# A planned single-core kernel: q and W1 loaded ahead of the filter, DFT angles built on VectorE, new planner numbers

## The chip, the cores and the metric

The kernel runs on one core of one Trainium2 chip. A core has five engines with an instruction queue each: TensorE (PE, with its weight loads as PEld), VectorE (DVE), ScalarE (ACT), GpSimd (POOL) and SyncE (SP), which here only issues transfers (DMAs). The metric is the device time of one execution in microseconds (us); less is better.

## What is computed

Two branches read x = q (2048 rows of 640, bfloat16) and are mixed by a gate. Branch A shifts k along the rows with a 4-tap filter, multiplies by v, convolves each column with a filter as long as the sequence (by FFT in the reference) and multiplies by q. Branch B is a layernorm, a matmul with W1, gelu, a shift of rows by column group, W2, a residual, another layernorm, and a W3-gelu-W4 block.

```python
g = _sigmoid((x * gate_w).sum(-1, keepdims=True))
kv = k_shift * v                                   # k_shift: 4 taps over k
y = irfft2(rfft2(pad(kv)) * rfft2(pad(ssm_k)))[:S] # long convolution
a = q * (y + kv * ssm_D)
h = _gelu(_layernorm(x) @ w1)
x1 = x + shifted(h) @ w2                           # column groups shifted by 1, -1, 2, -2 rows
b = x1 + _gelu(_layernorm(x1) @ w3) @ w4
return g * a + (1 - g) * b
```

## The kernel before

Rows are handled in 16 slabs of 128 (row = 16 p + slab). The long convolution is a DFT in two steps done as matmuls. Step 1 (line 783) multiplies the tables F1 (cosines and sines, interleaved by column) with a slab: first of the filter HT ("h1", 16 slabs by 2 halves), later of the product kv ("x1"). Step 2 (line 899) is a set of 64-wide matmuls with the small tables M3, after the data have been written to GHD or GXD in DRAM and read back in another layout; the spectra are multiplied on DVE (959), pass step 2 backwards into VD, and the inverse step 1 ("iv", 995) uses I1, the transposed F1.

The filter arrives as five tiles RG of 128 columns (line 400) and is transposed on PE (761); five evictions on ACT or DVE (379, 383) fill HT, and every step-1 matmul of the filter needs all five. HT shares its memory with KV: v of slabs 4c to 4c+3 may be loaded (859) only after step 1 of those slabs has read HT. The shifted-key products on DVE (870, 875, 879, 882) turn v into kv.

Branch B: for each slab statistics (on DVE 556 and 557, or on ACT 560 and 561, two passes with an accumulated sum), then on POOL the reciprocal root for a pair of slabs (573 to 579), then the normalisation on DVE (586), a transpose on PE (601), W1 (634) in four chunks of four slabs with five groups of five matmuls each and the gate's small matmuls (639, 643), gelu on ACT (652, 655), W2 (728), the residual on DVE (735), the second layernorm whose transposes are DMAs (593), W3 (815), gelu (819), W4 (827) and a residual (833).

The tables: F1[t1] holds cos and sin of an angle proportional to (column + 1) times row number. POOL writes index tables (432), DVE converts them (439), and for each of 16 t1 either DVE (453, one instruction of 256 columns) or POOL (456, two of 128) makes angle = column * row + offset, the offset 6144 or 4096 for the even and odd columns. DVE takes each group of four modulo 8192 (461), ACT takes the sine (463). M3 is made likewise by POOL and ACT (494 to 518).

Nothing is issued in written order. The function builds nodes, each with the engines that may run it and an assumed cost, and a planner (`Plan.schedule`) list-schedules them: each engine takes the node with the lowest rank, a rank being the latest start by the chain behind it, capped by the due times in the table PAR; it also picks the engine, the buffers and the PSUM slot (four slots ps0 to ps3). So any change of a cost or of PAR reorders all queues. Each engine then runs its queue strictly in that order, also where its first instruction has to wait.

Of the kernel before, what the change touches and what calls it, by code (L numbers as in the profile page):

```python
# [12 lines left out]
ALU = mybir.AluOpType  # L13
# [25 lines left out]
DMA_ISSUE = 60.0  # L39
# [185 lines left out]
def act_s(n):  # L225
    return 95.0 + 0.833 * n


def dve(n, r=1.04):
# [7 lines left out]
    "keep": (0.07,), "evac": (1.85,), "vpen": (43.36,), "mpen": (14.32,),  # L237
# [4 lines left out]
def kernel(  # L242
# [67 lines left out]
    BPI = big.tile([P, 1], F32, name="BPI")  # L310
# [115 lines left out]
    NANG = GEN[:, 0:8192].bitcast(I32)  # L426
    wci, wcf = gt_(256, I32), gt_(256, F32)
    oci, ocf = gt_(256, I32), gt_(256, F32)
# [5 lines left out]
    i_w = pl.add("iw", {G: 400}, iota_fn(wci, [[128, 2], [2, 64], [0, 2]], 1))  # L434
    i_s = pl.add("is", {G: 200}, iota_fn(s16i, [[1, T1]], 0, T1))
    i_o = pl.add("io", {G: 400}, iota_fn(oci, [[0, 2], [0, 64], [-2048, 2]], 6144))

    def vcopy(o, i):
        return lambda e: nc.vector.tensor_copy(out=o, in_=i)

    c_w = pl.add("cw", {V: 200}, vcopy(wcf, wci), [i_w])
    c_s = pl.add("cs", {V: 90}, vcopy(s16, s16i), [i_s])
    c_o = pl.add("co", {V: 200}, vcopy(ocf, oci), [i_o])
    m_bpi = pl.add("bpi", {V: 70}, lambda e: nc.vector.memset(BPI[:], -PI))
    f1n = []
    for g in range(4):
        st = []
        for j in range(4):
            t1 = 4 * g + j
            def f_ang(e, t1=t1):  # L450
                o = NANG[:, t1 * 256:(t1 + 1) * 256]
                if e == V:
                    nc.vector.scalar_tensor_tensor(out=o, in0=wcf, scalar=s16[:, t1:t1 + 1], in1=ocf, op0=ALU.mult, op1=ALU.add)
                else:
                    for x in range(2):
                        nc.gpsimd.tensor_scalar(out=o.rearrange("p (j c) -> p j c", c=2)[:, :, x],
                                                in0=wcf.rearrange("p (j c) -> p j c", c=2)[:, :, x], scalar1=s16[:, t1:t1 + 1],
                                                scalar2=6144.0 - 2048.0 * x, op0=ALU.mult, op1=ALU.add)
            st.append(pl.add("ang%d" % t1, {V: 397, G: 700}, f_ang, [c_w, c_s, c_o]))
        n1 = NANG[:, g * 1024:(g + 1) * 1024]  # L460
        an = pl.add("and%d" % g, {V: dve(1024, .6)}, lambda e, n1=n1: nc.vector.tensor_scalar(
            out=n1, in0=n1, scalar1=8191, scalar2=None, op0=ALU.bitwise_and), st)
        f1n.append(pl.add("sin%d" % g, {A: act_s(1024)}, lambda e, g=g, n1=n1: nc.scalar.activation(
            out=F1[:, :, 4 * g:4 * g + 4, :].rearrange("p h a c -> p a h c"),
            in_=n1.rearrange("p (a h c) -> p a h c", a=4, h=2), func=ACT.Sin,
            scale=PI / 4096, bias=BPI[:]), [an, m_bpi], mode="sin"))

# [24 lines left out]
    def f_m3c(e):  # L492
# [24 lines left out]
        out=sn3, in_=ani, func=ACT.Sin, scale=PI / 8, bias=BPI[:]), [m3b, m_bpi], mode="sin")  # L517
# [24 lines left out]
    n_misc = pl.add("misc", {G: 600}, f_misc)  # L542
# [7 lines left out]
    def ln_slab(i, s, dep):  # L550
        s0 = s & ~1

        def f_st(e):
# [4 lines left out]
            else:  # L558
                if i == 0:
                    nc.scalar.activation(out=JNK if i else JN0, in_=QX[:, s, :], func=ACT.Copy, accum_out=SSM[:, s:s + 1])  # L560
# [482 lines left out]
```

## Time and profile before

| | us |
|---|---|
| median of 3 runs (lowest, highest) | 255.62 (255.55, 255.73) |
| the profiled execution | 254.59 |
| its span, first to last instruction | 252.8 |
| PE busy | 223.6 |
| DVE busy | 194.6 |
| ACT busy | 154.2 |
| POOL busy, all of it in the first 100 us | 59.3 |

A busy time is the time in which an engine had an instruction running. In rows of the timeline the columns are start, duration, engine, line, operation, output and input, and in brackets the idle time before it and what ended that. SPq is the queue of transfers.

### The profile page before, as it was taken

How to read it: one execution, taken by the hardware profiler on the slowest of the kernel's cores; microseconds unless marked ns; L12 is line 12 of the kernel's file. 1: busy time of each engine (PE TensorE's matmuls, PEld its weight loads, DVE VectorE, ACT ScalarE, POOL GpSimd, SP SyncE). 2: the span in 40 equal slices, each digit the busy share in tenths (PEclk: the TensorE clock that was granted, in tenths of full speed). 3: DMA queues.
4: the chain of work that ended last, by engine and by line, in shares of the span. 5: the costliest groups of instructions: out<-in, count | busy, mean ns of one | idle time of the engine just before them, and what ended most of it. 6: DMA issues, size and time to landing. Idle time of an engine off the chain costs nothing.

```text
span 252.8 us, 4384 instructions
## 1 busy us (share of the span) xinstructions
PE 223.6 (88%) x1628; PEld 129.9 (51%) x1645; DVE 194.6 (77%) x308; ACT 154.2 (61%) x210; POOL 59.3 (23%) x144
## 2 busy tenths in 40 slices
PE   3858949999799999898698999969899999999993
PEld 3816535575467644664344446525334554557662
DVE  5889779996999999969987117876829785147995
ACT  2689949996579865676486564576868457231000
POOL 8899884122434880000000000000000000000000
PEclk9986997999999999999799999997999999999999
DMA  7998972279999962189999869958999243799973
GB/s 261 389 363 283 356 269 90 52 221 393 370 202 174 263 265 26 37 200 327 367 385 306 327 210 243 299 184 264 370 352 392 80 164 107 240 367 337 396 232 136
DMA packets 50069, 65.10 MB, mean 258 GB/s; under 512 B 19584, under 2 KB 36737, under 8 KB 49664
## 3 DMA queue, kind: packets, MB, share of 16 engines
q1 hardware_dynamic: 50048, 64.82, 80.1%
q8 instruction: 13, 0.21, 0.3%
q14 instruction: 8, 0.07, 0.1%
HBM read 37.03 MB, written 18.35 MB: 219 GB/s over the span
## 4 chain that ended last, share of the span: by engine, by line
PE 52%; DVE 14%; DMA 13%; ACT 12%; issue 5%; POOL 2%; DVEq 0%; ACTq 0%
PE PS L827 16%; PE PS L815 14%; PE PS L728 6%; PE PS L783 5%; DMA RK<-GXD 4%; PE PS L899 4%; DMA RK<-GHD 4%; DVE RK L1000 3%; PE PS L634 3%; PE PS L761 2%; DMA KV<-in_A_v_dram 2%; DMA CJ<-in_A_q_dram 2%; DVE QX L833 2%; ACT KV L379 1%; DMA RG<-in_A_ssm_k_dram 1%
## 5 line engine op out<-in xcount | busy, mean ns | idle before, releaser
L827 PE MATMUL PS<-W,RG 128*128 128x320 bf16 x384 | 54.9, 299 | 1.7 <-ACT RG L819 0.8
L815 PE MATMUL PS<-XNT,W 128*128 128x512 bf16 x229 | 53.2, 379 | 0.8 <-ACT SX L379 0.2
L379 ACT CAST SX<-PS 128x640 bf16<-128x640 f32 (+1 forms) x54 | 39.6, 769 | 20.2 <-PE PS L899 13.3
L827 PEld LDWEIGHTS <-RG 128*128 128x128 bf16 x384 | 37.2, 98 | 19.7 <-issue 5.3
L819 ACT ACTIVATE RG<-PS 128x1024 bf16<-128x1024 f32 x24 | 24.5, 1021 | 23.9 <-PE PS L815 21.2
L815 PEld LDWEIGHTS <-W 128*128 128x128 bf16 x240 | 23.0, 98 | 29.3 <-issue 3.4
L783 PE MATMUL PS<-KV,F 128*128 128x320 bf16 x128 | 26.7, 337 | 9.4 <-ACT KV L379 3.4
L383 DVE CAST SX<-PS 128x640 bf16<-128x640 f32 (+1 forms) x30 | 26.6, 911 | 5.1 <-PE PS L899 4.6
L634 PE MATMUL PS<-XNT,R 128*128 128x512 bf16 x94 | 24.1, 392 | 1.3 <-DVE XNT L383 1.0
L728 PE MATMUL PS<-R 128*128 128x320 bf16 x160 | 23.2, 299 | 1.9 <-DVE QX L735 1.5
L959 DVE TENSOR_TENSOR SX<-SX,R 128x2048 bf16<-128x2048 bf16 x20 | 23.5, 1219 | 0.5 <-PE PS L899 0.5
L833 DVE SCALAR_TENSOR_TENSOR QX<-PS,ZG,QX 128x640 bf16<-128x640 f32 x16 | 14.1, 882 | 12.4 <-PE PS L827 12.2
L783 PEld LDWEIGHTS <-F 128*128 128x128 bf16 x128 | 13.4, 107 | 15.6 <-issue 9.0
L586 DVE TENSOR_SCALAR XN<-QX,MV,RS 128x640 bf16<-128x640 bf16 x32 | 13.8, 454 | 8.5 <-DMA XNT<-XN 4.4
L1000 DVE SCALAR_TENSOR_TENSOR RK<-PS,ZG,CJ 128x640 bf16<-128x640 f32 x16 | 13.6, 879 | 8.4 <-PE PS L995 6.2
L728 PEld LDWEIGHTS <-R 128*128 128x128 bf16 x160 | 15.6, 98 | 8.6 <-issue 2.5
L879 DVE TENSOR_TENSOR RK<-RK 128x1280 bf16<-128x1280 bf16 x24 | 19.7, 822 | 0.4
L385 DVE TENSOR_SCALAR R<-PS 128x1024 bf16<-128x1024 f32 x10 | 11.8, 1218 | 10.2 <-PE PS L899 10.2
L875 DVE TENSOR_TENSOR RK<-RK,CJ 128x1280 bf16<-128x1280 bf16 x24 | 19.3, 819 | 0.0
L379 ACT CAST KV<-PS 128x1024 bf16<-128x1024 f32 x18 | 17.7, 1027 | 0.0
L899 PEld LDWEIGHTS <-M 64*64 64x64 bf16 x320 | 8.7, 109 | 16.8 <-issue 9.7
L749 ACT ACTIVATE QX<-QX,ZG 128x640 bf16<-128x640 bf16 x14 | 11.3, 828 | 9.4 <-DVE XN L586 9.4
(96 smaller groups left out, 283.5 us busy)
## 6 DMA issues: line engine op xcount, KB each, us to landing
GHD<-SX SPq DMA_DIRECT2D x8, 640.0 KB, 5.2
GXD<-SX SPq DMA_DIRECT2D x8, 640.0 KB, 6.3
RK<-GHD SPq DMA_DIRECT2D x4, 1280.0 KB, 8.6
R<-R SPq DMA_DIRECT2D x8, 640.0 KB, 8.2
RK<-GXD SPq DMA_DIRECT2D x4, 1280.0 KB, 9.3
VD<-KV SPq DMA_DIRECT2D x4, 1280.0 KB, 8.4
RK<-VD SPq DMA_DIRECT2D x8, 640.0 KB, 5.5
W<-in_B_w_dram SPq DMA_DIRECT2D x2, 1920.0 KB, 12.4
```

Of the source, the lines that this page charges most:

```text
L379: nc.scalar.copy(out=o, in_=i)
L383: nc.vector.tensor_copy(out=o, in_=i)
L634: nc.tensor.matmul(ps(pb)[:, j, :], lhsT=lhsT, rhs=XNT[:, xb.idx, k, :], start=(k == 0), stop=(k == DT - 1))
L728: nc.tensor.matmul(ps(pb)[:, j, 0:DH], lhsT=gst_ap(k, s), rhs=W2[:, k, j * DH:(j + 1) * DH], start=(k == 0), stop=(k == DT - 1))
L783: nc.tensor.matmul(ps(pb)[:, j, 0:DH], lhsT=F1[:, h, s, :], rhs=src[:, s, ds], start=True, stop=not dterm)
L815: nc.tensor.matmul(ps(pb)[:, j, :], lhsT=W3[:, k, (f0 + j) * P:(f0 + j + 1) * P], rhs=XNT[:, xb.idx, k, :], start=(k == 0), stop=(k == DT ...
L819: gns.append(pl.add("g2.%d.%d" % (c, f0), {A: act_p(1024)}, lambda e, f0=f0, pb=pb, gb=gb: nc.scalar.activation(out=GTP[:, gb.idx, f0 % 4: ...
L827: nc.tensor.matmul(ps(pb)[:, j, 0:DH], lhsT=GTP[:, gbs[f // 4].idx, f % 4, i * P:(i + 1) * P], rhs=W4[:, f, j * DH:(j + 1) * DH], start=(f ...
L875: m = pl.add("km%d.%d.%d" % (c, u, j), {V: dve(2 * D, .52)}, lambda e, src=src, cj=cj, tb=tb: nc.vector.tensor_tensor(out=TMP[:, tb.idx].r ...
L879: prev = pl.add("ka%d.%d.%d" % (c, u, j), {V: dve(2 * D, .52)}, lambda e, tb=tb: nc.vector.tensor_tensor(out=acc, in0=acc, in1=TMP[:, tb.i ...
L959: nc.vector.tensor_tensor(out=PQ[:, qb.idx], in0=XS[:, sb.idx].unsqueeze(1).to_broadcast([P, 2, 1024]), in1=HH[:, hhb.idx, u], op=ALU.mult)
L1000: nc.vector.scalar_tensor_tensor(out=GY[:, yb.idx].rearrange("p (j d) -> p j d", j=2), in0=ps(pb)[:, :, 0:DH], scalar=G32[:, s:s + 1], in1 ...
```

## The change

1. **Angles.** Only the sine angle, half a table (16 x 128 columns), is made, on DVE alone (`ang`, one instruction per t1, then `and`, 512 columns per group). The cosine is folded: ACT makes |angle - 4096| (`abs`), and takes sin(pi/2 - that * pi/4096) for the even columns and sin(angle * pi/4096 - pi) for the odd ones, two instructions of 512 elements where one of 1024 stood. The offset index table goes, the column table halves; BPI gets three columns of constants.
2. **Zero row of the shifted key** (`kz`): may be a DVE memset of 960 words; it was a POOL memset of 1920 half-words. Two loads of k no longer wait for it.
3. **Statistics.** ACT's two passes of the first layernorm scale by 1/640 themselves, so POOL drops one instruction in each such pair.
4. **Planner.** Assumed costs: 350 instead of 60 ns for issuing a DMA, 200 instead of 95 for an ACT instruction on SBUF, others for POOL, for the first transposes and the gate matmuls. A step-1 slab waits for its own group's two sine nodes. All numbers in PAR are new.

```diff
-DMA_ISSUE = 60.0
+DMA_ISSUE = 350.0
 def act_s(n):
-    return 95.0 + 0.833 * n
+    return 200.0 + 0.833 * n
 PAR = {
-    "trh": (-602.97, -1.2), "W1": (-11.87, 12.07, -4.15), "h1": (-36.96, 5.52), "W2": (1.53, 2.52),
+    "trh": (136.05, 12.4), "W1": (-14.71, 15.65, -7.45), "h1": (-32.59, 5.01), "W2": (-9.35, 3.4),
...
-            def f_ang(e, t1=t1):
-                o = NANG[:, t1 * 256:(t1 + 1) * 256]
-                if e == V:
-                    nc.vector.scalar_tensor_tensor(out=o, in0=wcf, scalar=s16[:, t1:t1 + 1], in1=ocf, op0=ALU.mult, op1=ALU.add)
...
-        f1n.append(pl.add("sin%d" % g, {A: act_s(1024)}, lambda e, g=g, n1=n1: nc.scalar.activation(
+                nc.vector.tensor_scalar(out=NANG[:, t1 * P:(t1 + 1) * P], in0=wcf, scalar1=s16[:, t1:t1 + 1], scalar2=None,
+                                        op0=ALU.mult)
+        an = pl.add("ang%d" % g, {V: 4 * dve(P, .6)}, f_ang, [c_w, c_s])
+        n1, n2 = NANG[:, g * 512:(g + 1) * 512], NABS[:, g * 512:(g + 1) * 512]
+        an = pl.add("and%d" % g, {V: dve(512, .6)}, lambda e, n1=n1: nc.vector.tensor_scalar(
+            out=n1, in0=n1, scalar1=8191, scalar2=None, op0=ALU.bitwise_and), [an])
+        ab = pl.add("abs%d" % g, {A: act_s(512)}, lambda e, n1=n1, n2=n2: nc.scalar.activation(
+            out=n2, in_=n1, func=ACT.Abs, scale=1.0, bias=BPI[:, 2:3]), [an, m_bpi])
+        for x, (src, dep) in enumerate(((n2, ab), (n1, an))):
+            f1n.append(pl.add("sin%d.%d" % (g, x), {A: act_s(512)}, lambda e, g=g, x=x, src=src: nc.scalar.activation(
+                out=F1[:, :, 4 * g:4 * g + 4, :].rearrange("p h a (j c) -> p a h j c", c=2)[:, :, :, :, x],
+                in_=src.rearrange("p (a h j) -> p a h j", a=4, h=2), func=ACT.Sin,
+                scale=-PI / 4096 if x == 0 else PI / 4096, bias=BPI[:, 1:2] if x == 0 else BPI[:, 0:1]), [dep, m_bpi], mode="sin"))
...
-            lds.append(pl.add("kz", {G: 300}, lambda e, kb=kb: nc.gpsimd.memset(KRG[0:1, kb.idx, 0:3, :], 0.0), [], [kb]))
+            lds.append(pl.add("kz", {V: 580, G: 1800}, lambda e, kb=kb: (nc.vector if e == V else nc.gpsimd).memset(
+                KRG[0:1, kb.idx, 0:3, :].rearrange("p t d -> p (t d)").bitcast(I32), 0), [], [kb]))
```

What this does to the queues. First comes SP's queue at its start: RG is the filter, QX is q (two slabs to a load), R_72 is W1, W_75 the filter's diagonal term. Before:

```order
L400 DMA RG<-in_A_ssm_k_dram 128x2048 x5
L403 DMA W_75<-in_A_ssm_D_dram 1x640
L396 DMA QX<-in_A_q_dram 128x1280 x2
L398 DMA R_72<-in_B_w_dram 128x5x640
L396 DMA QX<-in_A_q_dram 128x1280 x6
```

and now:

```order
L396 DMA QX<-in_A_q_dram 128x1280 x2
L398 DMA R_72<-in_B_w_dram 128x5x640
L400 DMA RG<-in_A_ssm_k_dram 128x2048 x5
L396 DMA QX<-in_A_q_dram 128x1280 x2
L403 DMA W_75<-in_A_ssm_D_dram 1x640
L396 DMA QX<-in_A_q_dram 128x1280 x4
```

The first four slabs of q and all of W1 moved ahead of the filter. Next comes ACT's queue at its start: the lines write F_79 (sines into F1), KV (here the transposed filter HT, from PSUM), SX (step-1 results), and take statistics of QX. Before:

```order
L463 ACT_TABLE_LOAD
L463 ACTIVATE F_79<-W_75,BPI 128x4x2x128
L379 COPY KV<-PS_65 128x16x128
L379 COPY KV<-PS_63 128x16x128
L379 COPY KV<-PS_64 128x16x128
L463 ACTIVATE F_79<-W_75,BPI 128x4x2x128
L379 CAST SX<-PS_63 128x640
L379 CAST SX<-PS_65 128x640
```

and now (L458 is `abs`, L461 the half sines, L558 and L560 the two statistics passes):

```order
L458 ACTIVATE W_75<-W_75,BPI 128x512
L461 ACT_TABLE_LOAD
L461 ACTIVATE F_79<-W_75,BPI 128x4x2x64
L558 ACTIVATE R_72,MV<-QX 128x640
L560 ACTIVATE R_72,ST<-QX 128x640
L461 ACTIVATE F_79<-W_75,BPI 128x4x2x64
L458 ACTIVATE W_75<-W_75,BPI 128x512
L461 ACTIVATE F_79<-W_75,BPI 128x4x2x64 x2
L379 COPY KV<-PS_63 128x16x128
L458 ACTIVATE W_75<-W_75,BPI 128x512
L461 ACTIVATE F_79<-W_75,BPI 128x4x2x64 x2
L458 ACTIVATE W_75<-W_75,BPI 128x512
```

Seven of the eight half sines and the statistics of a slab now stand among the filter's evictions, and there is a second table load.

On PE, the first step-1 matmul of the filter followed the five filter transposes directly; now two pairs of layernorm transposes stand among those five, and W1's first chunk (25 matmuls and the gate's) behind them, ahead of step 1. That chunk stood behind 18 step-1 matmuls. Of the statistics, three instead of four of the first slabs are on DVE. Further down, W3's first six groups stand ahead of the last four W2 slabs (slabs 14, 15, 0 and 1) instead of behind them; from the first step-1 matmul of kv on, PE's queue has the same groups in nearly the same order, with u, the five column blocks of step 2, counted downwards.

More of the change, by code (lines that the diff above doesn't have):

```diff
@@ L309 @@
     ONE1 = big.tile([1, P], BF16, name="ONE1")
-    BPI = big.tile([P, 1], F32, name="BPI")
+    BPI = big.tile([P, 3], F32, name="BPI")
     ST = big.tile([P, T1, 12], F32, name="ST")
@@ L442, with f_bpi @@
     c_s = pl.add("cs", {V: 90}, vcopy(s16, s16i), [i_s])
-    c_o = pl.add("co", {V: 200}, vcopy(ocf, oci), [i_o])
-    m_bpi = pl.add("bpi", {V: 70}, lambda e: nc.vector.memset(BPI[:], -PI))
+    def f_bpi(e):
+        nc.vector.memset(BPI[:, 0:1], -PI)
+        nc.vector.memset(BPI[:, 1:2], PI / 2)
+        nc.vector.memset(BPI[:, 2:3], -4096.0)
+    m_bpi = pl.add("bpi", {V: 190}, f_bpi)
     f1n = []
     for g in range(4):
-        st = []
-        for j in range(4):
-            t1 = 4 * g + j
-            def f_ang(e, t1=t1):
-                o = NANG[:, t1 * 256:(t1 + 1) * 256]
-                if e == V:
[L453 to L466, printed above, removed]
@@ L516 @@
     m3s = pl.add("m3s", {A: act_s(3 * MB)}, lambda e: nc.scalar.activation(
-        out=sn3, in_=ani, func=ACT.Sin, scale=PI / 8, bias=BPI[:]), [m3b, m_bpi], mode="sin")
+        out=sn3, in_=ani, func=ACT.Sin, scale=PI / 8, bias=BPI[:, 0:1]), [m3b, m_bpi], mode="sin")
     m3n = pl.add("m3n", {G: 1200}, lambda e: [nc.gpsimd.tensor_tensor(
```

50 lines of the change are left out of this document (27 added, 23 removed), and 4 rows, old and new, of the table PAR.

## Prediction

> **What bounds the kernel now.** I read the page's busy shares first, then the windows by stage, then what VectorE (DVE) waits for, then the chain that ended last, and last the timeline of the first 40 us.
>
> ```profile
> PE 223.6 (88%) x1628; PEld 129.9 (51%) x1645; DVE 194.6 (77%) x308; ACT 154.2 (61%) x210; POOL 59.3 (23%) x144
> 0.00:40.00 40.00, 27.27 (x213) 18.59 (x216) 32.18 (x76) 27.72 (x42) 34.47 (x96) 0.88 0.88 316
> 40.00:113.00 73.00, 69.71 (x488) 42.49 (x492) 68.17 (x122) 56.73 (x91) 24.86 (x48) 1.00 0.69 187
> ```
>
> The window rows give busy us of PE, PEld, DVE, ACT, POOL in that order, then the granted clock, the DMA share and GB/s. From 40 to 113 us PE and DVE are both nearly full (69.7 and 68.2 of 73); after that PE alone is, with 223.6 - 97.0 = 126.6 of the last 139.8 us. Only the first 40 us have room: PE sits idle 12.7 us, DVE 7.8 us, and POOL, a helper that should be slack, is busy 34.5. So the change can gain in the head, and whether the gain lives depends on whether DVE, full afterwards, starts its long middle earlier.
>
> What DVE lost in the head is in its own rows (start, duration, idle before it, and who ended it):
>
> ```profile
> 0.79 0.06 DVE L444 MEMSET BPI<- 128x1 f32 x1 [0.79 <-PEq L1027]
> 2.25 1.85 DVE L439 CAST W<-W 128x256 f32<-128x256 int32 x3 [1.40 <-POOL W L432]
> 6.08 0.70 DVE L461 TENSOR_SCALAR W<-W 128x1024 int32<-128x1024 int32 x1 [0.67 <-POOL W L456]
> 11.96 0.69 DVE L461 TENSOR_SCALAR W<-W 128x1024 int32<-128x1024 int32 x1 [0.75 <-POOL W L456]
> 18.42 0.80 DVE L586 TENSOR_SCALAR XN<-QX,MV,RS 128x640 bf16<-128x640 bf16 x2 [0.50 <-POOL RS L579]
> 27.96 0.80 DVE L586 TENSOR_SCALAR XN<-QX,MV,RS 128x640 bf16<-128x640 bf16 x2 [0.63 <-POOL RS L579]
> 30.63 0.80 DVE L586 TENSOR_SCALAR XN<-QX,MV,RS 128x640 bf16<-128x640 bf16 x2 [0.67 <-POOL RS L579]
> 33.16 0.85 DVE L586 TENSOR_SCALAR XN<-QX,MV,RS 128x640 bf16<-128x640 bf16 x1 [1.73 <-POOL RS L579]
> 39.44 0.45 DVE L586 TENSOR_SCALAR XN<-QX,MV,RS 128x640 bf16<-128x640 bf16 x1 [0.18 <-POOL RS L579]
> 39.81 0.82 DVE L870 TENSOR_TENSOR RK<-RK,CJ 128x1280 bf16<-128x1280 bf16 x1
> ```
>
> The idle sums to 7.3 us: 0.8 at the start, and 6.5 that all end on POOL (first its index tables, then its angles, then the layernorm's reciprocal roots queued behind them). At 39.81 DVE starts the first shifted-key product, and from there it is saturated. That instruction is my **anchor**.
>
> **The change, part by part.**
>
> *Angles.* These rows price the old and bound the new:
>
> ```profile
> L456 POOL TENSOR_SCALAR W<-W 128x128 int32<-128x128 f32 x16 | 8.3, 521 | 1.3
> L453 DVE SCALAR_TENSOR_TENSOR W<-W 128x256 int32<-128x256 f32 x8 | 3.8, 525 | 0.0
> L461 DVE TENSOR_SCALAR W<-W 128x1024 int32<-128x1024 int32 x4 | 2.8, 688 | 1.4 <-POOL W L456 1.4
> L514 DVE TENSOR_SCALAR I<-I 128x192 int32<-128x192 int32 x1 | 0.3, 253 | 0.0
> L463 ACT ACTIVATE F<-W,BPI 128x1024 bf16<-128x1024 int32 x4 | 4.6, 1150 | 4.8 <-DVE W L461 4.8
> L516 ACT ACTIVATE I<-I,BPI 128x192 f32<-128x192 int32 x1 | 0.5, 454 | 0.0
> L849 POOL MEMSET RK<- 1x1920 bf16 x1 | 1.7, 1687 | 0.1
> ```
>
> A line through the 192- and 1024-wide DVE rows (253 and 688 ns) gives 0.22 us for 128 columns and 0.42 for 512. DVE now does 16 x 0.22 + 4 x 0.42 = 5.2 us for angles instead of 8 x 0.525 + 4 x 0.688 = 7.0. POOL loses 8.3 us of angles, the 1.7 us zero-fill and about 0.8 of index table: 10.8 us of its 34.5. The same line through the two sine rows (454 and 1150 ns) gives 0.72 us for 512: ACT has twelve such instructions, 8.7 us, for four at 1.15, 4.6: **+4.1 us on ACT**, plus one more table load.
>
> The zero-fill is now a DVE memset of 960 words; no row shows one. It lies between 0.06 (the bias memset above) and 1.69 (POOL's); I take 1.0, half of POOL's count for half the elements, near the upper row.
>
> *DVE up to the anchor.* Beside the angles (-1.8) and about -0.8 for halved index casts, the order puts there: the zero-fill (+1.0), two bias memsets (+0.1), one more slab's statistics (two passes and an aggregate, a cadence of +1.0) and one more filter eviction (+1.2). Sum +0.8 us. Two step-1 evictions and two normalisations, 2.2 us, now come after the anchor; they are owed, not saved. So the lead of DVE at equal work is 7.3 - 0.8 (start) - 0.8 (more work) - X = **5.7 - X**, X being its idle in the new head.
>
> *X.* The queue of loads is now q (2), W1, filter (5). This fixes the first work of PE:
>
> ```profile
> 4.21 7.69 PE L761 MATMUL PS<-IDN,RG 128*128 128x128 bf16 x80 [4.21 <-DMA RG<-in_A_ssm_k_dram]
> 20.00 2.83 PE L783 MATMUL PS<-KV,F 128*128 128x320 bf16 x10
> 24.80 1.24 PE L634 MATMUL PS<-XNT,R 128*128 128x512 bf16 x4 [0.99 <-DVE XNT L383]
> 29.49 2.32 PE L634 MATMUL PS<-XNT,R 128*128 128x512 bf16 x9
> 10.00:15.00 5.00, 1.90 (x31) 1.78 (x29) 4.15 (x14) 5.00 (x3) 4.49 (x12) 1.00 1.04 392
> ```
>
> At 392 GB/s the 1.44 MB of q and W1 put the first filter piece 3.7 us later, at 7.9, and the last at about 13.3. The five filter transposes (16 in about 1.8 us) with two layernorm transposes between them then end near 19 us instead of 11.9; W1's first chunk follows (25 matmuls at 0.22 and the gate, 6 us) and ends near 25, where the old program began it at 24.80 and ended it at 31.8. The old program had done 18 step-1 matmuls by then (the row at 20.00 has ten of them in 2.83 us, at a clock below full; at 0.16 each they are 2.9), so PE is some 3 us ahead at 25 us.
>
> The first two normalisations need POOL's roots: statistics of slabs 0 and 1 end near 7.4, the root near 8.5, and DVE, busy with other statistics and angles, comes to them at 9.6. POOL's 5 us of mask tables runs at 12 to 17, ahead of the next roots but before their statistics, which need q pieces landing near 14 to 15. Walking DVE's queue so, I find it waiting 0.3 to 0.7 us before the anchor; I take **X = 1.7**, a us more, for PE at less than full clock and for ACT being late. Lead: 4.0 us.
>
> *ACT.* It is the tight engine of the new head: in my walk it hardly rests from 5 to 36 us, and its eviction of the last filter transpose comes near 22 us, behind thirteen sines, absolutes and statistics. Step 1 starts at 25 on PE, so 3 us of cover remain.
>
> ```profile
> 45.41 1.28 ACT L463 ACT_TABLE_LOAD   x1
> 46.71 1.15 ACT L463 ACTIVATE F<-W,BPI 128x1024 bf16<-128x1024 int32 x1
> ```
>
> A load costs 1.30 us to the next instruction; the extra one stands ahead of the first sine, and that I have counted. The Trainium skill, ScalarE: Activation LUTs, section What ACT_TABLE_LOAD costs, gives 2.66 us for a switch, the load and as much again of drain; these two rows show no drain. By the page the first sine would come 1.4 us later and the sum would be up to 1.4 us worse.
>
> *Middle.* The lead is carried, since DVE is full, but it must pass one transfer:
>
> ```profile
> 108.59 0.53 SPq L859 DMA_DIRECT2D KV<-in_A_v_dram  x1
> 113.71 0.82 DVE L882 TENSOR_TENSOR KV<-RK,KV 128x1280 bf16<-128x1280 bf16 x1 [1.55 <-DMA KV<-in_A_v_dram]
> ```
>
> The last piece of v is issued behind the transposed stores of the second layernorm in SP's queue, which wait for DVE; both orders have it there, so it goes out 4 us earlier with DVE, and the key chain, the read of GHD and the stage behind it follow. The first W3 group now stands ahead of four W2 slabs; that reorders full engines and I cost it at nothing (it covers the 0.8 us PE waited for the first W4; without such cover it costs that).
>
> *End.* The second half has the same rows with small swaps. Two of them lose cover:
>
> ```profile
> 158.17 0.63 PE L899 MATMUL PS<-RK,M 64*64 64x512 bf16 x8
> 158.62 1.22 PE L899 MATMUL PS<-SX,M 64*64 64x512 bf16 x16
> ...
> 168.33 1.06 PE L899 MATMUL PS<-RK,M 64*64 64x512 bf16 x16 [1.26 <-DMA RK<-GHD]
> 213.93 3.42 PE L827 MATMUL PS<-W,RG 128*128 128x320 bf16 x24
> 217.19 6.64 PE L815 MATMUL PS<-XNT,W 128*128 128x512 bf16 x29
> 217.98 7.32 SPq L983 DMA_DIRECT2D RK<-VD  x5
> 223.66 1.79 PE L995 MATMUL PS<-RK,I 128*128 128x320 bf16 x12
> RK<-VD SPq DMA_DIRECT2D x8, 640.0 KB, 5.5
> ```
>
> Between the last read of an input buffer and this wait for GHD one product of eight small matmuls (158.17 to 158.62) fewer now stands: +0.45. Between the last of those products and the inverse step, 4 W3 groups (217.19 to 223.66 is three of them) and a W4, 4 x 2.16 + 3.42 = 12.1, become 2 and 2, 11.2; the inverse began 0.2 us after 217.98 + 5.5, so +0.7. The sum is -4.0 + 0.45 + 0.7 = **-2.9 us**: span 252.8 to 249.9, the profiled execution 254.59 to 251.7. The median of the runs, 255.62, lies 1.03 above that execution; with the same distance, 252.7.
>
> **The rivals.**
>
> *More than that.* X near 0.3 and no lost cover: -5.4, about 250; with the 0.8 of the first W4, 249.4. For it: POOL ended all of the head's idle, and it is relieved of a third. Against: ACT.
>
> *ACT takes POOL's place.* If instructions of 0.72 really cost 0.9 (the POOL and DVE rows of 0.52 are that much above the line) and evictions slip by 2 to 3 us, X is 4 to 5 and the result -0.2 to +0.6: 255.4 to 256.2.
>
> *Slower: PE at half clock in W1.* PE now sits idle to 7.9 us instead of 4.2, and W1's first chunk comes into the head where gaps are many.
>
> ```profile
> 38.12 2.34 PE L634 MATMUL PS<-XNT,R 128*128 128x512 bf16 x5
> 46.24 1.24 PE L634 MATMUL PS<-XNT,R 128*128 128x512 bf16 x5
> 35.00:40.00 5.00, 3.64 (x21) 2.00 (x20) 4.75 (x13) 3.42 (x6) 3.73 (x10) 0.72 0.52 174
> ```
>
> The same five matmuls took 2.34 us after a gap (granted clock 0.72 in that window) and 1.24 later. If all 25 run so, W1 ends 5.4 us later, at 30.5; X becomes 7.1, the lead -1.4, the end +2.5: 258.1. It decides once the slow clock costs more than 2.9 us there, more than half of the 25. Against it: the transposes ahead of W1 run for 8 us with gaps under 1 us in my walk, and the old ones after 4 us of idle ran in windows of clock 1.00. The Trainium skill, TensorE: Matmul & The Clock Gate, section on the HAM clock gate, says that an idle window of about 3.4 us halves the clock and as long a busy one restores it; by that rule the transposes warm the array and W1 is spared, which leaves the sum as it is.
>
> *It doesn't do what it says.* DVE's 0.22 us angles could run at 0.5, as the 128-wide ones did on POOL: +4.7 us of DVE work, some of it where DVE now idles; with X near 0.5 the end is about +0.4 to -1.
>
> **How the numbers follow.** Forecast (-1.5 to -5): 0.50. More: 0.14. ACT: 0.14. Half clock, in part or whole (+0.3 to +4): 0.17. Dear angles: 0.05. A measurement of this kernel tells 0.2% (0.5 us) from no change. Faster: 0.50 + 0.14 + 0.05 of ACT + 0.03 of dear angles = 0.72; slower: 0.15 of half clock and 0.03 of ACT = 0.18; the rest, 0.10, the same. The range leaves out the far ends of "more" and of "half clock": 248.8 to 257.0.
>
> **What would show it.** Right: DVE's first shifted-key product near 34 us with no idle ended by POOL before it; W1's first matmul near 19; angle rows of 0.2 us on DVE and 0.7 on ACT; the last v load issued near 104.6. Wrong: DVE or PE idle in the head ended by ACT sums to over 4 us, or W1's first 25 matmuls take over 9 us, or the lead is there at 113 us and gone at the inverse step, which would put the fault in the second half's swaps, that I priced at 1.2 us.

## The result, and the profile after

| | before | after |
|---|---|---|
| median, us (lowest, highest) | 255.68 (255.55, 256.73) | 248.51 (247.80, 250.63) |
| ratio of the times, with its 95% interval | | 0.9725 (0.9659 to 0.9790) |
| the profiled execution, us | 254.59 | 248.14 |
| its span, us | 252.8 | 246.3 |

The change makes the kernel 7.2 us faster by the medians. 2.9 were forecast: direction right, size not. The first row of the page of after has the busy shares:

```profile
PE 219.0 (89%) x1645; PEld 127.6 (52%) x1645; DVE 191.9 (78%) x320; ACT 158.0 (64%) x216; POOL 44.8 (18%) x122
```

POOL lost 14.5 us of work, DVE 2.7, and ACT gained 3.8. These totals do not say where the 6.5 us of the span come from. For that I cut both spans at two DVE instructions: the **anchor** (first shifted-key product) and the last product of the shifted key with v (line 882 before, 884 after), after which all of kv is there. Windows of before, in the columns used above (length, then PE, PEld, DVE, ACT, POOL):

```profile
0.00:39.81 39.81, 27.08 (x212) 18.43 (x215) 31.99 (x76) 27.54 (x41) 34.47 (x96) 0.88 0.89 318
39.81:120.45 80.64, 76.13 (x523) 46.23 (x529) 74.96 (x132) 61.21 (x98) 24.86 (x48) 0.99 0.72 200
120.45:252.80 132.35, 120.41 (x894) 65.20 (x901) 87.61 (x102) 65.45 (x72) 0.00 (x0) 0.97 0.83 274
```

and of after:

```profile
0.00:33.41 33.41, 23.02 (x215) 16.24 (x216) 30.50 (x86) 29.45 (x46) 22.15 (x76) 0.90 0.92 318
33.41:113.92 80.51, 77.02 (x518) 45.93 (x516) 77.84 (x138) 61.09 (x97) 22.63 (x46) 1.00 0.81 228
113.92:246.30 132.38, 118.96 (x914) 65.42 (x913) 83.58 (x98) 67.46 (x76) 0.00 (x0) 1.00 0.82 273
```

The third rows are equal in length, 132.35 and 132.38: the second half gave and took nothing in these two executions (before's is 1.0 us below its median; the table of the runs below shows that its second half is a short one). The whole 6.5 us stand before it, and DVE's column splits them. Up to the cut DVE works 30.50 + 77.84 = 108.3 us instead of 31.99 + 74.96 = 107.0, so 1.4 more. It idles 2.9 us in the head instead of 7.8, and 2.7 in the middle instead of 5.7. So 4.9 us of idle time went in the head and **3.0 in the middle**, less 1.4 of work: 6.5. The head I had forecast; the middle's 3.0 us are what the runs have to explain. Before's two longest waits of DVE there are 1.85 us for a gelu, ahead of the copy of a gate column, and 1.55 for the last piece of v (the row at 113.71 in the prediction):

```profile
60.35 0.16 DVE L660 COPY ZG<-PS 128x4 f32<-128x4 f32 x1 [1.85 <-ACT R L655]
```

In after the first is gone, the second has shrunk to 0.29, and one of 0.85 is new:

```profile
46.79 0.82 DVE L736 SCALAR_TENSOR_TENSOR QX<-PS,QX 128x640 bf16<-128x640 f32 x1 [0.85 <-ACT RG L560]
106.81 0.82 DVE L884 TENSOR_TENSOR KV<-RK,KV 128x1280 bf16<-128x1280 bf16 x1 [0.29 <-DMA KV<-in_A_v_dram]
```

What DVE still waits for in the new head, in its timeline (the rows with idle time):

```profile
0.79 0.06 DVE L444 MEMSET BPI<- 128x1 f32 x1 [0.79 <-PEq L1029]
1.07 0.86 DVE L850 MEMSET RK<- 1x960 int32 x1 [0.16 <-issue]
27.30 0.45 DVE L587 TENSOR_SCALAR XN<-QX,MV,RS 128x640 bf16<-128x640 bf16 x1 [0.68 <-PE PS L602]
27.90 0.82 DVE L383 COPY XNT<-PS 128x1280 bf16<-128x1280 bf16 x1 [0.15 <-PE PS L602]
30.04 0.82 DVE L383 COPY XNT<-PS 128x1280 bf16<-128x1280 bf16 x1 [0.52 <-PE PS L602]
...
33.41 0.82 DVE L872 TENSOR_TENSOR RK<-RK,CJ 128x1280 bf16<-128x1280 bf16 x1
```

No idle time ends on POOL any more; before, 6.5 us did.

### The profile page after: what moved, and what is told of

Read it like the earlier page. It is cut to its first block, busy times and chain, and to the rows that moved or that the text cites. A ratio compares the mean times of both kernels' runs of the same rounds, so it can differ in the third digit from the quotient of the medians.

```text
span 246.3 us, 4416 instructions
## 1 busy us (share of the span) xinstructions
PE 219.0 (89%) x1645; PEld 127.6 (52%) x1645; DVE 191.9 (78%) x320; ACT 158.0 (64%) x216; POOL 44.8 (18%) x122
## 4 chain that ended last, share of the span: by engine, by line
PE 33%; DMA 11%; ACT 4%; DVE 4%; issue 1%; DVEq 0%
PE PS L828 16%; PE PS L816 10%; DMA RK<-GXD 5%; DMA RK<-GHD 4%; PE PS L901 3%; PE PS L997 3%; DMA CJ<-in_A_q_dram 2%; DVE QX L834 1%; PE PS L784 1%; ACT SX L379 1%; ACT R L381 1%; DVE R L385 1%; ACT RG L820 1%; ACT KV L379 1%; DVE RK L1002 1%
## 5 line engine op out<-in xcount | busy, mean ns | idle before, releaser
L816 PE MATMUL PS<-XNT,W 128*128 128x512 bf16 x240 | 54.3, 379 | 0.4
L379 ACT CAST SX<-PS 128x640 bf16<-128x640 f32 (+1 forms) x57 | 42.3, 780 | 14.7 <-PE PS L901 8.7
L383 DVE CAST SX<-PS 128x640 bf16<-128x640 f32 (+1 forms) x27 | 23.7, 892 | 9.6 <-ACT RG L820 5.7
L784 PE MATMUL PS<-KV,F 128*128 128x320 bf16 x128 | 24.9, 313 | 6.1 <-ACT F L461 1.5
L729 PE MATMUL PS<-R 128*128 128x320 bf16 x160 | 23.7, 299 | 0.2 <-ACT R L653 0.2
L635 PE MATMUL PS<-XNT,R 128*128 128x512 bf16 x100 | 23.1, 382 | 0.0
L784 PEld LDWEIGHTS <-F 128*128 128x128 bf16 x128 | 12.7, 101 | 13.6 <-issue 6.5
L901 PE MATMUL PS<-RK,M 64*64 64x512 bf16 x160 | 13.6, 387 | 4.6 <-DMA RK<-GHD 1.4
L560 ACT ACTIVATE RG<-QX 128x640 bf16<-128x640 bf16 x16 | 11.8, 738 | 8.6 <-DVE QX L736 8.4
L379 ACT CAST KV<-PS 128x1024 bf16<-128x1024 f32 x17 | 17.1, 1042 | 0.0
```

The source lines that it names most:

```text
L379: nc.scalar.copy(out=o, in_=i)
L635: nc.tensor.matmul(ps(pb)[:, j, :], lhsT=lhsT, rhs=XNT[:, xb.idx, k, :], start=(k == 0), stop=(k == DT - 1))
L729: nc.tensor.matmul(ps(pb)[:, j, 0:DH], lhsT=gst_ap(k, s), rhs=W2[:, k, j * DH:(j + 1) * DH], start=(k == 0), stop=(k == DT - 1))
L784: nc.tensor.matmul(ps(pb)[:, j, 0:DH], lhsT=F1[:, h, s, :], rhs=src[:, s, ds], start=True, stop=not dterm)
L816: nc.tensor.matmul(ps(pb)[:, j, :], lhsT=W3[:, k, (f0 + j) * P:(f0 + j + 1) * P], rhs=XNT[:, xb.idx, k, :], start=(k == 0), stop=(k == DT ...
L901: nc.tensor.matmul(pt[64 * C:64 * C + 64, R, :], lhsT=M3[64 * R:64 * R + 64, m, :], rhs=rhs_fn(R, C), start=start, stop=stop)
```

## The experiments

To change one thing at a time the order must not be planned anew. In most runs a list gives each engine its nodes in sequence, and the planner only hands out buffers. With the list of its own order such a kernel is the same program as the planned one.

```diff
+def force(nodes):
+    where = {nm: (e, i) for e in ORDER for i, nm in enumerate(ORDER[e].split())}
...
-                        if bk is not None and k >= bk:
+                        if n.rank != nxt[e]:
                             break
```

In the lists km, ka and kv are the shifted-key products, their sums and the product with v; h1 is a step-1 slab of the filter, he its eviction; xn a normalisation, te the eviction of its transposes, st statistics, add a residual behind W2, xo a scaling of q, g1 a gelu behind W1, m3s the sine of M3, misc and m3i POOL's constants and mask tables, h0 to h4 the filter's loads. Ratios are to the kernel before on the same chip (medians 256.2 to 256.9 us), so 0.01 is 2.6 us. Single executions lie up to 2.4 us from the median of their run, a few up to 3.8 above it, and most intervals are 0.3 to 0.6% wide each way. A trace shows one execution, so its lengths can be off by as much; ratios are of medians.

### Which stretch of the order

The order of one kernel up to an instruction, then what is left in the order of the other:

```diff
 after's code:   head_new       after's order to the first km0.0.3 (anchor), then before's
 after's code:   head_mid_new   after's order to the load v3, then before's
 before's code:  head_old       before's order to the anchor, then after's
 before's code:  tail_new       before's order to the load v3, then after's
```

The new head alone:

> The code of after; engine and place of every piece of work are given by a list: up to DVE's first shifted-key product the order of after, from there on what is left in the order of before (same engines as before). Theory 'carried' (the prediction): the head is worth 4.2 us and is carried, the later order is worth nothing in the middle and costs 1.2 us in the second half, so this is the best of all, 255.7 - 4.2 = 251.5 us, and the 7.1 us of the result stay unexplained. Theory 'middle' (the new order between 33 and 105 us removes DVE waits that before had, some 2.4 us): also about 251.5 here, since those waits come back. Theory 'head only' (a head that is early by itself removes the later waits too): 248.5 or less.

Measured: 0.9861 (0.9814 to 0.9907), 3.6 us less than before. The head is worth about what I gave it; "head only" falls.

> The code of after, the order of after up to the issue of the last load of v, what is left in the order of before. Carried: as the head alone, 251.5 us. Middle: 251.5 - 2.4 = 249.1, and 1 us less than that (248) if the swaps of the second half cost what I priced, so no slower than after, 248.5. Head only: 248 as well, but then equal to the run with the new head alone.

Measured: 0.975 (0.9709 to 0.9790), 6.4 us less: the order of the middle is worth 2.8 us behind the new head, give or take 1.6 by the two intervals.

> The code of before (full table, POOL's angles), its order up to DVE's first shifted-key product, what is left in the order of after. Carried: the head is old, so 255.7 + 0 + 1.2 = 256.9 us. Middle: 255.7 - 2.4 - 0.5 (what else the second half showed) = 252.8 to 253.3. Head only: 255.7 or more.

Measured: 1.0114 (1.0073 to 1.0155), 2.9 us more than before. No theory had this: behind the old head the new order of the rest loses. Its value is no property of its own but of its fit to what stands ahead. Part of the loss may come from the join of the two orders, which is in neither kernel.

> The code of before, its order up to the issue of the last load of v, what is left in the order of after. Carried: +1.2 for the two lost covers, 256.9 us. Middle: 255 to 256.8, the second half being worth at most 0.5 us of gain. If the second half's order is what made the result, it is 253 or less here.

Measured: 0.9955 (0.9927 to 0.9984), 1.2 us less. The new second half costs nothing; if anything it gains. The 1.2 us that I charged for lost cover fall here.

### Which part of the middle

After's order to the last W2 group ahead of W3, some 66 us, and before's behind it:

```diff
 PE, after:        ... W2.12 h1.12.0 h1.12.1 W2.13 | W3.0.0 to W3.0.10 W2.14 ...
+PE, upto_w3_new:  ... W2.12 h1.12.0 h1.12.1 W2.13 | W2.14 W2.15 h1.13.0 h1.13.1 W2.0 W2.1 W3.0.0 to W3.0.10 ...
```

> The code of after, its order up to the last W2 group that it has ahead of W3 (some 66 us), what is left in the order of before: so W2's last four slabs stand again ahead of W3's first six groups, and the residuals on DVE and the gelus on ACT behind them too. Measured so far: the new head alone 3.6 us less than before, head and middle up to the last v load 6.4 less. If the swap of W3 and W2 (which I priced at nothing) makes the middle's 2.8 us, this gives 3.6 less (ratio 0.986, the last v load issued near 104.5); if the waits between 33 and 66 us make it (DVE for the third gate slab 1.4 to 1.8, PE for a residual 1.5), 6.4 less (0.975, the last v load near 101.5). An even split gives 0.980.

Measured: 0.974 (0.9699 to 0.9782), 6.7 us less. By the medians all of the middle's gain is made between the anchor and 66 us, and W3 ahead of W2 is worth nothing, as priced. The windows from the anchor to the last product with v show how; first of head_new, then of upto_w3_new:

```profile
32.98:116.44 83.46, 77.29 (x517) 46.67 (x522) 76.94 (x136) 59.36 (x96) 22.62 (x46) 1.00 0.77 221
```

```profile
33.56:114.85 81.29, 76.92 (x518) 46.69 (x522) 77.09 (x136) 61.47 (x98) 24.22 (x46) 1.00 0.79 223
```

DVE has the same work (76.94 and 77.09) and idles 6.5 us in the one and 4.2 in the other. Two things limit this reading. The traced execution of head_new is 2.4 us above the median of its run, that of upto_w3_new 0.6. And head_new's longest wait stands at the join of the two orders, in neither kernel, so its 3.6 us may be too little for the head and the 2.8 too much for the middle:

```profile
36.92 0.82 DVE L383 CAST SX<-PS 128x640 bf16<-128x640 f32 x1 [2.03 <-ACT SX L379]
```

Next, single waits. In head_new DVE waited 1.4 us to copy the last gate column (node z3) out of PSUM, behind a gelu and its table load:

```diff
 DVE: te0.3.2 add4 he.8.0 ka0.1.1
-     z3
      ka0.1.0 xn1.2 xn1.3 kv2
+     z3
      gate0 km1.0.3
```

> As the run with the new head alone (order of before from the first shifted-key product on), with one instruction of DVE moved: the copy of the gate column of the last W1 chunk, that waited 1.4 us for a gelu behind a table load with DVE's queue behind it, stands three instructions and a product later. If DVE's waits set the middle, 1.0 to 1.4 us less than 0.986, so 0.981, and the last v load at 103.3 instead of 104.5. If the wait is hidden (the next thing late takes its place), no change: 0.986.

Measured: 0.9819 (0.9781 to 0.9857). The wait went; 0.4% against head_new is within the intervals. Then a second one, at the join of the two orders:

```diff
 DVE: km0.0.3 he.3.1 xn0.11
-     he.6.0
      xn0.12 km0.0.2 km0.0.1 ka0.0.2
+     he.6.0
```

> As the run with the new head and the gate copy moved (0.9819), with one more DVE instruction moved: at the join of the two orders DVE stood 2.0 us at the eviction of a step-1 slab (34.6 to 36.6 us) that neither kernel waits for there; that eviction now stands behind two products and a sum. If DVE's waits between 33 and 66 us are what the middle is worth, up to 2.0 us less: 0.974 to 0.976, as much as the whole new order up to there (0.974), and the last v load near 101 to 101.5. If such waits are made up elsewhere, 0.982.

Measured: 0.9832 (0.9772 to 0.9892): nothing further. In its trace (an execution 2.8 us above the run's median) the wait at the join is gone, and DVE waits 2.63 us for transposes of PE at 42.35 instead. Taking out one or two waits does not give what the new order gives. The reverse in after:

```diff
 DVE: kv2 km1.0.3 add5
+     z3
      km1.0.2 km1.0.1
-     z3
```

> The kernel after with one DVE instruction moved the other way: the copy of the last gate column stands two products earlier, where by the trace of after its gelu ends 1.4 us after DVE comes to it. If a DVE wait at this place costs what it lasts, 1.1 to 1.5 us more than after: 0.977 to 0.979. If DVE has room, the same as after.

Measured: 0.9699 (0.9643 to 0.9756). This told nothing: the wait that it should make did not come, as the timeline shows (no idle time before the copy).

```profile
57.22 0.16 DVE L661 COPY ZG<-PS 128x4 f32<-128x4 f32 x1
```

Then a wait of PE in after, 1.5 us for the last half sine:

```diff
 ACT: te0.2.0 m3s
+     sin3.1
      te0.2.2 g1.1.2 g1.1.0 g1.2.4 he.4.1
-     sin3.1
      he.5.1
```

> The kernel after with one instruction of ACT moved: the last half sine (43.96 us, with a table load ahead of it, another for gelu behind it, and PE waiting 1.5 us for it) stands behind the sine of M3 at 36.8 us, under the table that is loaded there. Two loads (2.6 us) leave ACT and PE's 1.5 us wait goes. If such PE waits in the middle reach the end, 1.0 to 1.5 us less than after; if DVE, full from 33 to 110 us, sets the middle, 0 to 0.5 less (ratio to before 0.970 to 0.9725).

Measured: 0.974 (0.9687 to 0.9793), no gain. Beside these, on the chip of z3_early and two_waits_out:

> The kernel after, its order written out as a list, on the same chip as the three others: the reference for them and for the runs before. All theories: 0.9725 within its interval (0.966 to 0.979). Against the run with the new head and middle and the old tail (0.975): my prediction's lost covers would make this 1.2 us the slower of the two (0.980); no cost of the new tail gives 0.975 or less.

Measured: 0.9727 (0.9670 to 0.9784). The new tail is not the slower one.

### What made the head

First the angles alone, in before's order:

```diff
-DVE: ang0 ang2 ang3 and0      POOL: ang1 ang4 ang5 ang7 ...   ACT: sin0
+DVE: ang0 and0                POOL: none                      ACT: abs0 sin0.0 sin0.1
```

> Only the way the angles are made is new: half table on DVE, folded cosine on ACT (each group's absolute and two sines at the place of its one sine), in the order of before for all else, loads included; zero-fill on POOL as before. If the relief of POOL makes the head's lead (my reason), most of the 6.5 us that DVE waited for POOL goes: the first shifted-key product comes at 35 to 36 instead of 39.8 and the time is 2.5 to 4 us less. If ACT takes POOL's place (four more us of sines ahead of the filter's evictions) or the loads and PE's order make the lead, it comes at 38 to 40 and the time is within 1 us of before.

Measured: 0.9985 (0.9954 to 1.0015), nothing. POOL's waits did go, and others took their place. DVE's waits to 41 us (total, times, longest):

```profile
DVE KV L383 <- PE PS L762: 3.6, 2, 3.1
DVE XNT L383 <- PE PS L602: 1.4, 2, 1.2
```

DVE now waits for the filter's transposes, on PE first and loaded first. PE then waits for their evictions as long as it did in before (3.40 us there, ahead of its first step-1 matmul at 15.30), so step 1 begins no earlier, in its timeline:

```profile
15.71 0.30 PE L784 MATMUL PS<-KV,F 128*128 128x320 bf16 x1 [3.43 <-ACT KV L379]
```

PE's clock was also 0.50 for 13.7 us of this head, against 6.8 in the same place of before's trace; what that cost is not separated.

Then all of after's order, with the angles made as before:

```diff
-DVE: ang0 and0     ACT: abs0 sin0.0 sin0.1     POOL: misc m3i0
+DVE: ang0 ang2 ang3 and0     ACT: sin0         POOL: misc ang1 ang4 ang5 ang7 ang10 ang11 m3i0
```

> The other half of the angles' run: all of the order of after (loads, head, middle, tail), with the angles made as before, eight of the 16 on POOL at their old place ahead of the mask tables, full table, one sine for a group, zero-fill on POOL. The angles alone gave 0.9985. If the order alone makes the gain, 0.975 here. If the order needs POOL free (its 8.3 us of angles now stand ahead of the layernorm's first roots, which the new head wants at 9 us; the zero-fill 1.7), the first transposes of the layernorm wait some 5 us and the time is that of before or above: 0.99 to 1.01.

Measured: 0.9997 (0.9961 to 1.0033), nothing either. The waits, of DVE and of PE:

```profile
DVE XN L586 <- POOL RS L579: 4.3, 2, 3.1
DVE W L461 <- POOL W L456: 2.8, 2, 2.1
...
PE PS L601 <- DVE XN L586: 8.7, 2, 8.0
```

So neither half gives anything alone, and both together 7 us: by these waits the new order asks for normalised rows early, and only a free POOL can deliver them. Last, only the first eight loads of after put back:

```diff
 SP:
-q0 q1 w1 h0 h1 h2 h3 h4
+h0 h1 h2 h3 h4 q0 q1 w1
```

> The kernel after, with only SP's first eight loads changed: the filter's five ahead of the two of q and of W1 as before, every engine's order as in after. The filter's 2.62 MB at the 392 GB/s of the early windows put q 6.7 us later; the layernorm's transposes, second in PE's queue, wait for it. If the order of the loads carries the head's gain, 3 to 5 us more than after (first shifted-key product near 38 instead of 33.4): 0.985 to 0.992. If PE's order with POOL free carries it whatever comes first, within 1 us of after.

Measured: 0.9856 (0.9809 to 0.9903), the anchor at 36.53 instead of 33.4 to 33.5. The loads' order is worth 3.3 us.

### Whose time sets the middle

Three microseconds are added to DVE, to PE, and to PE in the second half, all in after:

```diff
 dve_plus3:      km1.0.3:  the product of line 872 made 5 times
 pe_plus3:       W2.9:     for k in list(range(DT)) * 3
 pe_plus3_late:  W4.10:    for f in list(range(FT)) * 2
```

> The kernel after; one shifted-key product of DVE (near 56 us) is made five times instead of once, the result unchanged: 4 x 0.74 = 2.96 us more work for DVE. If DVE's time between 33 and 110 us sets the end, 2.5 to 3 us more than after (249.36 beside before at 256.47, ratio 0.9727): 0.982 to 0.985. If DVE has room there, under 1 us more: 0.973 to 0.976.

Measured: 0.9892 (0.9829 to 0.9956), 4.2 us more than after_beside.

> The kernel after; one W2 slab (near 67 us, ten matmuls, 1.52 us by its rows) is computed three times instead of once into the same place: 20 x 0.145 = 2.9 us more for PE, nothing for the others. If DVE alone sets the middle, under 1 us more: 0.973 to 0.977. If PE, as full as DVE there by the windows (59.4 of 60 us from 50 to 110 us or so), sets it as well, 2 to 3 us more: 0.981 to 0.985.

Measured: 0.974 (0.9692 to 0.9789), 0.3 us more. Its traced execution, 1.3 us above the run's median, does reach the last product with v at 116.41, 2.2 us after after_beside's.

> The kernel after; one W4 slab of the second half (near 187 us, 24 matmuls, 3.42 us) is computed twice: 24 x 0.136 = 3.3 us more for PE. By my reading PE alone is full after 113 us, so 2.5 to 3.3 us more, 0.982 to 0.986; less if the waits for transfers set that half: under 1 us, 0.973 to 0.977.

Measured: 0.9797 (0.9744 to 0.9849), 1.8 us more for 3.3 added, with intervals that overlap. In its trace the second half takes 135.19 us against 132.20 in after_beside, 3.0 more, so waits hide little there. In the middle DVE's time sets the end; whether PE has room there is not shown (the interval leaves 1 to 2 us open, and the trace speaks against much). The window of dve_plus3 from the anchor to the last product with v, against 80.70 long and 77.80 busy in after_beside:

```profile
33.83:119.77 85.94, 79.00 (x512) 47.02 (x516) 81.29 (x141) 60.49 (x96) 22.10 (x46) 0.96 0.74 214
```

3.5 us more work, and idle time up from 2.9 to 4.7. PE is close behind: with pe_plus3 DVE has a new wait for W2.

```profile
DVE QX L736 <- PE PS L729: 2.0, 1, 2.0
```

Then work taken from DVE, given to ACT:

```diff
-DVE: he.7.1 he.9.1 xo10 xo11
+ACT: he.7.1 he.9.1 xo10 xo11
 dve_lighter2 also moves he.4.0 he.5.0 xe.2.0 xo2
```

> The kernel after with four instructions moved from DVE to ACT at the same place in time: two evictions of step-1 slabs (58.7 and 64.3 us, a cadence of 0.74 us each on DVE) and two scalings of q (102.8 us, 0.34 each): 2.2 us less work for DVE between 33 and 110 us, some 2.8 more for ACT, which has 53 of 72 us there. Three microseconds added to DVE cost 4.2 us. If the same holds downward, 1.5 to 2.2 us less than after: 0.964 to 0.967 of before (after 0.9727), faster than both kernels. If PE (a wait of 2 us on it appeared when it was given 2.9 us more) is as near to the end as DVE, 0 to 1 us less: 0.969 to 0.9727.

Measured: 0.9681 (0.9644 to 0.9717), median 247.62. It has the lowest median and ratio of all, 1.2 us under after_beside; the intervals overlap, so it isn't shown to beat after. Nor is the moved work shown to be the reason. DVE's work fell by 1.8 us and its idle time rose by 2.1, so the middle is no shorter; first after_beside, then dve_lighter:

```profile
33.50:114.20 80.70, 77.18 (x520) 46.07 (x518) 77.80 (x138) 61.27 (x97) 22.44 (x46) 1.00 0.78 228
```

```profile
32.05:113.07 81.02, 76.56 (x512) 45.45 (x510) 76.01 (x134) 63.62 (x102) 25.36 (x47) 1.00 0.82 233
```

What this execution has ahead it has at the anchor, 1.45 us, behind a head whose order is that of after and whose clock is 1.00 instead of 0.90 (see the last section).

> As the one before, with four more moved: the step-1 evictions at 42.2 and 44.4 us, one of kv at 107.6 us, and a scaling of q at 68.7 us, 4.8 us less for DVE in all. If DVE's time is all, 3 to 4.8 us less than after (0.954 to 0.961). If PE or ACT is next in line, no further gain over the run before, or a loss where ACT (9.95 of 10 us busy from 70 to 80 us) makes the evictions late: 0.964 to 0.975.

Measured: 0.9797 (0.9751 to 0.9843), 1.8 us more than after, with intervals that overlap. DVE now waits 4.2 us for W2, and PE 2.1 us for the last half sine on ACT (1.5 in after), so ACT's lateness passes through PE, as I read it:

```profile
DVE QX L736 <- PE PS L729: 4.2, 2, 4.0
```

### The runs side by side

DVE from the anchor to the last product with v, and the time from there to the end, from the window rows of one profiled execution each; the ratios are of medians.

| run | anchor | work | idle | last product | from there to the end | ratio |
|---|---|---|---|---|---|---|
| before | 39.81 | 75.0 | 5.7 | 120.45 | 132.35 | 1 |
| angles_only | 39.41 | 75.1 | 4.9 | 119.37 | 135.53 | 0.9985 |
| order_only | 42.07 | 77.6 | 1.7 | 121.36 | 133.84 | 0.9997 |
| head_new | 32.98 | 76.9 | 6.5 | 116.44 | 136.96 | 0.9861 |
| z3_later | 32.66 | 77.0 | 5.1 | 114.78 | 134.22 | 0.9819 |
| upto_w3_new | 33.56 | 77.1 | 4.2 | 114.85 | 134.25 | 0.9740 |
| head_mid_new | 32.20 | 76.9 | 3.9 | 113.00 | 134.80 | 0.9750 |
| after_beside | 33.50 | 77.8 | 2.9 | 114.20 | 132.20 | 0.9727 |
| filter_first | 36.53 | 77.8 | 3.3 | 117.69 | 133.21 | 0.9856 |
| dve_plus3 | 33.83 | 81.3 | 4.7 | 119.77 | 133.23 | 0.9892 |
| dve_lighter | 32.05 | 76.0 | 5.0 | 113.07 | 132.33 | 0.9681 |

The ratio goes more with the last product with v than with the anchor: head_new and after_beside start the middle within 0.5 us of each other and end it 2.2 apart. It does not go with it alone: angles_only and dve_plus3 reach it within 0.4 us of each other, and their ratios are 0.9% apart.

The last column varies too. With before's second half it is 134.2 to 137.0 us in five runs and 132.35 in before itself. With after's it is 132.1 to 133.2 in after and eight variants of it, and 133.8 to 134.3 in the three runs that make the angles as before did (order_only, head_old, tail_new). So the equal lengths in the traces of the two kernels do not show that the second half gave nothing. By the medians it may have given up to a microsecond: 0.3 and 0.6 us (upto_w3_new and head_mid_new against after_beside) and the 1.2 of tail_new, of which only the last is clear of the noise.

## Why the prediction was right in part and wrong in size

**Angles: right on DVE, low on ACT.** The groups of after:

```profile
L461 ACT ACTIVATE F<-W,BPI 128x512 bf16<-128x512 int32 x4 | 3.5, 881 | 0.0
L461 ACT ACTIVATE F<-W,BPI 128x512 bf16<-128x512 f32 x4 | 3.5, 880 | 0.1
L452 DVE TENSOR_SCALAR W<-W 128x128 int32<-128x128 f32 x16 | 3.5, 285 | 0.0
L458 ACT ACTIVATE W<-W,BPI 128x512 f32<-128x512 int32 x4 | 2.8, 710 | 2.2 <-DVE W L456 2.2
L456 DVE TENSOR_SCALAR W<-W 128x512 int32<-128x512 int32 x4 | 1.8, 450 | 0.1
L850 DVE MEMSET RK<- 1x960 int32 x1 | 0.9, 858 | 0.2 <-issue 0.2
```

Sixteen angles in 3.5 us are 0.22 each, as forecast; 512 columns took 0.45 (0.42), the zero-fill 0.86 (1.0). A half sine took 0.88, not 0.72: the size of the rival "ACT takes POOL's place". It did not come true: no DVE wait in the new head ends on ACT, and PE's waits that do sum to 1.95 us, under the 4 that I had named as the sign of it.

**The head: right.** Anchor at 33.41, forecast near 34, no wait for POOL ahead of it. The lead at the anchor is 6.4 us less the 2.9 of work that is owed (I had 2.2): 3.5, forecast 4.0. Behind before's later order the head gave 3.6 us (head_new). The angles' part in it is as I said only behind the new loads and PE order; each half alone gave nothing, which I had not foreseen.

**PE in the head: too slow in the forecast.** The timeline of after:

```profile
8.34 1.93 PE L762 MATMUL PS<-IDN,RG 128*128 128x128 bf16 x16 [8.34 <-DMA RG<-in_A_ssm_k_dram]
...
11.12 1.25 PE L762 MATMUL PS<-IDN,RG 128*128 128x128 bf16 x16
...
13.39 3.17 PE L762 MATMUL PS<-IDN,RG 128*128 128x128 bf16 x48 [0.18 <-ACT KV L379]
16.48 3.83 PE L635 MATMUL PS<-XNT,R 128*128 128x512 bf16 x17
```

The filter came at 8.34 (forecast 7.9). Sixteen transposes took 1.93 us once and 1.1 to 1.25 then, where I put 1.8 for each (my own row, 80 in 7.69 us, gives 1.54), so W1 began at 16.48 and not near 19. What the earlier start was worth at the anchor is not shown. The rival "half clock in W1" did not come: the clock is 1.00 there.

**The middle: the step that failed.** I wrote that "the lead is carried, since DVE is full", and costed the reordering at nothing. My own row said 68.17 of 73 us, so 4.8 us idle, and an idle engine on the path is where an order can gain. From the anchor to the last product with v it was 5.7, and the new order left 2.7. The last load of v, forecast for 104.6, went out here, in SP's queue:

```profile
101.98 0.53 SPq L861 DMA_DIRECT2D KV<-in_A_v_dram  x1
...
113.92 0.82 DVE L884 TENSOR_TENSOR KV<-RK,KV 128x1280 bf16<-128x1280 bf16 x1
```

Shown: 3.0 us of DVE's idle time left the middle (the windows of the two kernels), the gain is one of order (head_new against head_mid_new), the order loses behind the old head (head_old), and DVE's time counts there (dve_plus3). The medians put the gain between 33 and 66 us (upto_w3_new), but the join in head_new blurs that: upto_w3_new's trace still waits 1.42 us for the last v, which after does not. Not shown: which moves make it. Two single waits, taken out one after the other, did not add up to it. I read it so that the new order always has a product at hand for DVE while PE and ACT catch up, but that is argued from the shrinking idle time alone.

**The second half: the other step that failed.** +0.45 and +0.7 for lost cover; the length of that part came out the same in the two traces, and its order cost nothing in tail_new (1.2 us less than before) and after_beside; it rather gains. The two places in PE's timeline:

```profile
161.53 1.06 PE L901 MATMUL PS<-RK,M 64*64 64x512 bf16 x16 [1.45 <-DMA RK<-GHD]
...
215.00 1.25 PE L997 MATMUL PS<-RK,I 128*128 128x320 bf16 x8
```

The wait for GHD grew from 1.26 to 1.45, 0.2 and not 0.45. The inverse step began without a wait, 4.6 us after its read was issued at 210.37, where I had counted the group's median of 5.5.

The sum for the span: 2.9 forecast, + 3.0 for the middle, + 1.15 for the second half, - 0.5 for the lead gives 6.5. The median lies 0.4 us above the profiled execution this time and 1.1 in the measurement of before beside it, which makes 7.2. The case "more than that" had nearly this size, but for another reason: it put it in the head (X near 0.3; DVE idled 2.1 us there beside the start) and in covers that hold, of which only the second was so.

Three slips of the forecast changed little. The terms of DVE's extra work add up to 0.7, not 0.8. With X of 4 to 5, "ACT takes POOL's place" comes to -0.55 to +0.45, not -0.2 to +0.6. And 0.2% is too fine for what a run tells here: the intervals are 0.3 to 0.7% wide each way.

## What to carry to other kernels

An engine that is 93% busy on the path is not full: its 7% of idle time is the first thing that a new order can take, so list those waits and price them like any other term. The same order can gain 2.8 us behind one head and lose behind another, and two edits that are worth nothing alone can be worth 7 us together; an edit that frees one engine should be priced with the order that uses the freedom. To find which engine sets a stretch, add the same time to each in turn: for DVE the answer was clear of the noise, where moving single waits had said nothing; for PE three microseconds were too few.

## What the hardware showed unasked

The clock was halved without a long pause of PE. In after one wait of 1.00 us stands ahead of it, from 23.5 to 24.5 us; a second of 0.77 begins at 25.8, with the clock already down. In PE's timeline:

```profile
24.52 0.30 PE L784 MATMUL PS<-KV,F 128*128 128x320 bf16 x1 [1.00 <-ACT R L653]
...
26.57 1.22 PE L602 MATMUL PS<-IDN,XN 128*128 128x128 bf16 x10 [0.77 <-ACT R L656]
```

and in its windows of a microsecond (length, PE busy, granted clock):

```profile
23.00:24.00 1.00, 0.52 (x3) 1.00 1.01 184
24.00:25.00 1.00, 0.48 (x3) 1.00 0.75 236
25.00:26.00 1.00, 0.80 (x3) 0.50 0.97 396
...
31.00:32.00 1.00, 1.00 (x4) 0.59 0.62 168
32.00:33.00 1.00, 1.00 (x18) 1.00 1.00 383
```

From 25 to 31.8 us the clock is 0.50, though PE is busy without a gap from 26.6 on. Ten transposes take 1.22 us in place of 0.72, twice, and the products between them 1.27 and 1.80 where sine_early, at clock 1.00, has 0.70 and 1.03: 2.3 us of PE in all.

The order of the head does not decide this alone. Eleven kept executions have after's order up to 36 us at least. In five of them the clock is halved here for 6.8 us (after, after_beside, z3_early, dve_lighter2, dve_plus3), in three for 3.4 (pe_plus3, pe_plus3_late, upto_w3_new) and in three not at all (sine_early, dve_lighter, head_mid_new). The lengths, from the granted clock in windows of 0.2 us, are 3.41 to 3.42 or 6.82 to 6.83 us, in the heads of before, head_new and z3_later too, and 13.65 in angles_only: one, two or four times 3.41. The anchor comes at 33.4 to 33.8 us after 6.8 us of half clock, at 33.0 to 33.6 after 3.4, and at 32.1 to 32.8 after none, so it seems to cost about a microsecond there. Whether that reaches the end is not shown: dve_lighter has the lowest time of all, but sine_early is no faster than after.

The Trainium skill, TensorE: Matmul & The Clock Gate, section Part 1: The HAM clock gate (the "warmup" mystery), says that an idle window of about 3.4 us throttles the array. The length agrees with these traces. But no such window was idle here: in after PE was busy without a gap from 16 to 23 us, then half of two microseconds was idle, and that sufficed. In dve_lighter the microseconds from 25 to 27 were 52% and 43% busy and the clock stayed at 1.00, so how much idle time it takes stays open.
